# Gathering an expert's tokens in blocks of 32 slots and turning them on VectorE, in an attention and expert-routing kernel

## The chip, the cores and the metric

The kernel runs on one core of a Trainium2 chip. The metric is the device time of one execution in microseconds. The profile is one execution recorded by the hardware profiler. Engine names in it: PE is TensorE's matrix multiply, PEld its weight load, DVE is VectorE, ACT is ScalarE, POOL is GpSimd, SP is SyncE (a trailing q is that engine's queue of DMA issues and waits).

## What is computed

Two blocks follow each other. The first is attention with a threshold, for 8 batches of 8 heads of 576 positions of 64 numbers; its output is laid out as 4608 tokens of 512 numbers (8 heads beside each other). The second sends each token to one of 8 experts, picked by a hash of its id, and puts it through two matrix products.

```python
scores = scale * np.matmul(q, k.transpose(0, 1, 3, 2))
thresh = np.max(scores, axis=-1, keepdims=True) - tau
scores = np.where(scores >= thresh, scores, -1000000000.0)
attn = np.exp(scores - np.max(scores, axis=-1, keepdims=True))
attn = attn / (np.sum(attn, axis=-1, keepdims=True) + 1e-09)
x = np.matmul(attn, v)              # then to (4608, 512)
expert_idx = token_ids * np.int64(2654435761) % np.int64(8)
for e in range(8):
    xe = x[expert_idx == e]
    out[expert_idx == e] = np.maximum(xe @ w1[e], 0.0) @ w2[e]
```

All of it is float32; w1[e] is 512 x 1024 and w2[e] is 1024 x 512. With these inputs the experts get 598, 596, 571, 565, 599, 533, 570 and 576 tokens.

## The kernel before

*Attention* walks over 32 pairs of heads: 4 head pairs (`hp`), each for 8 batches, head pair outermost. A pair has five steps (`s` 0 to 4), and `n = 5 * pair + s` counts them to `LAST` = 160. The order of the instructions inside a step is written out by hand. A step computes scores on TensorE (L214), negates them and takes their minimum on VectorE (`negate`, L225), adds the threshold on GpSimd (`thr`, L232), takes the exponential on ScalarE (L239), masks and sums on VectorE (`mask`, L250), and one to two steps later turns the weights on TensorE (L261) and multiplies with v (L292). At step 0, two pairs later, `put_xm` (L331) divides by the sums on VectorE, and SyncE's queue writes the pair's 576 rows of 128 columns to memory (L337, L342): into `xa_scratch` (columns of the first three head pairs, 384 wide) or `xb_scratch` (the fourth, 128 wide).

*Routing* runs in small pieces between attention's steps. `route` gives each token a slot: expert e owns CAP = 610 slots. `scatters` writes the token numbers into two slot tables in memory (L478), loads them back (L488) and merges them on VectorE (L494) into `gidx`: for each expert five columns of token numbers, one column for each tile of tokens (three of 128 rows, two of 113). A table entry without a token holds a large number, which the gathers pass over.

*Gathers.* `fetch` brings the rows of one tile of one expert from `xa_scratch` or `xb_scratch` into a buffer `xg` by an indirect DMA issued from GpSimd (L104), tokens on partitions. The `xa` parts of experts 0 and 1 are fetched between attention's steps from step `G0` = 130 on, when all writes to `xa_scratch` have been issued. The `xb` parts of both follow the last attention step.

*Turning.* The first product needs the 512 features on partitions. For expert 0 this is done at the end of attention (`early_xT`, L545), and its first product is started there (`early_h`, `late_h`). For experts 1 to 7 `turn_x` does it: four TensorE transposes a tile into PSUM (L722) and one VectorE copy to `xT` (L724).

*Experts.* For each expert e: `gemm1` (L731; 8 groups of 2 x 4 matmuls with 305 tokens as columns; its ReLU goes by turns to ScalarE, L737, and VectorE, L739); then the load of w1 and the ten gathers for expert e+2 (whose buffers are free again); then the second product of e, among which the turns of expert e+1 are spread. `gemm2_last` (L757) computes the last 226 slots with features on partitions, `gemm2` (L745) the first 384 with tokens on partitions, and `turn_last` (L768) turns the former back on TensorE. Each tile of output is copied by ScalarE (L773) and scattered to its rows of the output by an indirect DMA from GpSimd (`store`, L774), each waiting for the one before, as all write the same tensor at places known only at run time. Tokens over an expert's capacity would go through a loop at the end; with these inputs it runs zero times.

The order around the change, in the expert loop, is:

```python
gemm1(e)
load_w1(e + 2); fetch tiles of e + 2
turn_x(e + 1, 0); turn_x(e + 1, 1)
gemm2_last(e)
for kt in range(3):
    turn_x(e + 1, kt + 2)
    gemm2(e, kt)
    turn_last(3 + kt)   # kt = 0, 1
load_w2(e + 2)
```

Of the kernel before, what the change touches and what calls it, by code (L numbers as in the profile page):

```python
# [20 lines left out]
def kernel(  # L21
# [34 lines left out]
    KT, KF, TL = 5, 3, 113  # L56
    TROWS = [P] * KF + [TL] * (KT - KF)
    FIRST = [sum(TROWS[:k]) for k in range(KT)]
    CAP = sum(TROWS)
# [9 lines left out]

    slot_dram = [nc.dram_tensor(f"slot_scratch_{i}", (NSLOT, 1), I32, kind="Internal").ap()  # L70
                 for i in range(2)]

    XA = DIN - P
    xa_dram = nc.dram_tensor("xa_scratch", (N, XA), FP32, kind="Internal").ap()
    xb_dram = nc.dram_tensor("xb_scratch", (N, P), FP32, kind="Internal").ap()
# [16 lines left out]
    drop = consts.tile([P, 1], FP32, name="drop")  # L92
    gidx = consts.tile([P, E, KT], I32, name="gidx")
    gidx_odd = consts.tile([P, E, KT], I32, name="gidx_odd")
# [3 lines left out]
    xg_bufs = [consts.tile([P, DIN], FP32, name=f"xg_{i}") for i in range(2 * KT)]  # L98
# [4 lines left out]
    def gather(x_dram, dst, idx):  # L103
        nc.gpsimd.indirect_dma_start(  # L104
            out=dst, out_offset=None, in_=x_dram[:, :],
            in_offset=bass.IndirectOffsetOnAxis(ap=idx, axis=0),
            bounds_check=N - 1, oob_is_err=False)

    def fetch(e, kt, part):
        xg = xg_bufs[(e * KT + kt) % (2 * KT)]  # L110
        dram, dst = (xa_dram, xg[:, 0:XA]) if part == 0 else (xb_dram, xg[:, XA:DIN])
        gather(dram, dst, gidx[:, e, kt:kt + 1])

    def load_w1(e):
        w1_sb = w_pool.tile([P, CO, F], FP32, name="w1_sb")
        nc.sync.dma_start(out=w1_sb[:], in_=w1[e].rearrange("(c p) f -> p c f", p=P))
        w_tiles[e, 1] = w1_sb
# [6 lines left out]
    with tc.tile_pool(name="a_q", bufs=1) as a_q, \  # L124
# [188 lines left out]
        def x_place(p):  # L313
            hp, b = divmod(p, B)
            return (xa_dram, b * S, hp * P) if hp < HP - 1 else (xb_dram, b * S, 0)
# [10 lines left out]
        def put_xm(p):  # L326
# [9 lines left out]
            x_dram, r0, c0 = x_place(p)  # L336
# [136 lines left out]
        placed = []  # L473

        def scatters():

            for c in range(NTC):
                nc.gpsimd.indirect_dma_start(  # L478
                    out=slot_dram[c % 2][:, :],
                    out_offset=bass.IndirectOffsetOnAxis(ap=slot_i[:, c:c + 1], axis=0),  # L480
                    in_=tok[:, c:c + 1], in_offset=None, bounds_check=NSLOT - 1,
                    oob_is_err=False)
                yield
            for _ in range(4):
                yield
            for table, dst in zip(slot_dram, (gidx, gidx_odd)):
                for p0, p1, k in ((0, TL, KT), (TL, P, KF)):
                    nc.sync.dma_start(  # L488
                        out=dst[p0:p1, :, 0:k],
                        in_=bass.AP(tensor=table.tensor, offset=p0 * KT,  # L490
                                    ap=[[k, p1 - p0], [CAP, E], [1, k]]))
            for _ in range(4):
                yield
            nc.vector.tensor_tensor(out=gidx[:], in0=gidx[:], in1=gidx_odd[:], op=ALU.min)  # L494
# [31 lines left out]
        def constants():  # L526
# [7 lines left out]
            nc.gpsimd.memset(gidx_odd[:], BIG)  # L534
# [4 lines left out]
        def early_xT(tr, k0, k1, c0, c1):  # L539
# [8 lines left out]
            for ka, kb in ((k0, min(k1, KF)), (max(k0, KF), k1)):  # L548
# [43 lines left out]
        G0 = NS * ((HP - 1) * B + 2)  # L592
        pieces, scatter_pieces = route(), scatters()
# [6 lines left out]
        with tc.manual_schedule():  # L600
# [7 lines left out]
            for n in range(LAST + NS + 1):  # L608
# [13 lines left out]
                if s == 1 and 3 <= p < 2 + len(xg_bufs):  # L622
                    nc.sync.dma_start(out=xg_bufs[p - 2][:], in_=xg_bufs[0][:])
                q = p - 1
# [67 lines left out]

                g = n - G0
                if 0 <= g < 2 * KT:
                    fetch(g // KT, g % KT, 0)
                if n == LAST:
                    fill(1)
            for g in range(2 * KT):
                fetch(g // KT, g % KT, 1)
# [6 lines left out]
    with tc.tile_pool(name="m_x", bufs=1) as m_x, \  # L706
# [7 lines left out]
        o_bufs = [m_o.tile([P, DIN], FP32, name=f"o_{i}") for i in range(KT)]  # L714
        oT_sb = m_o.tile([P, CO, CAP - FIRST[KF]], FP32, name="oT_sb")
# [48 lines left out]
        def turn_last(kt, idx):  # L764
            o_ps = ps_x.tile([P, CO, P], FP32, name="xT_ps")
            s0 = FIRST[kt] - FIRST[KF]
            for co in range(CO):
                nc.tensor.transpose(o_ps[0:TL, co, :], oT_sb[:, co, s0:s0 + TL], ident[:])  # L768
            store(o_ps[:].rearrange("p c d -> p (c d)"), kt, idx, TL)
# [8 lines left out]
        def turn_x(e, kt):  # L778
            put_xT(xg_bufs[(e * KT + kt) % (2 * KT)], xT_bufs[e % 2], kt, TROWS[kt])

        with tc.manual_schedule():
            for e in range(E):
                if e > 0:
                    gemm1(w_tiles.pop((e, 1)), xT_bufs[e % 2], h_bufs[e % 2], 2, CH)
                if e + 2 < E:
                    load_w1(e + 2)
                    for g in range(2 * KT):
                        fetch(e + 2, g // 2, g % 2)
                w2_sb = w_tiles.pop((e, 2))
                if e + 1 < E:  # L790
                    turn_x(e + 1, 0)
                    turn_x(e + 1, 1)
                gemm2_last(w2_sb, h_bufs[e % 2])
                for kt in range(KF):
                    if e + 1 < E:
                        turn_x(e + 1, kt + 2)
# [8 lines left out]
        with tc.For_i(0, n_ov, 1) as it:  # L805
# [15 lines left out]
            gather(xa_dram, xg_bufs[0][:, 0:XA], idx[:, 0:1])  # L821
            gather(xb_dram, xg_bufs[0][:, XA:DIN], idx[:, 0:1])
# [37 lines left out]
```

## Time and profile before

| | before |
|---|---|
| time, median of 3 | 1026.33 us (1025.42 to 1027.76) |
| span of the profiled execution | 1025.3 us |
| TensorE clock granted, mean | 0.996 |
| busy: PE, DVE, ACT, POOL | 98%, 49%, 44%, 31% of the span |
| attention, to its last write issued | about 475 us |
| one expert, gemm1 to gemm1 (L731 of experts 1 and 2) | 536.02 to 604.70 us |
| TensorE transposes of turn_x (L722) | 140, busy 19.1 us |
| copies of turned tokens (L724) | 35, busy 22.6 us |
| gathers (L104), experts 0 to 7 | 80, about 1.0 us each on GpSimd |
| stores (L774) | 40, 0.98 us each on GpSimd |

The profile's page has a line of busy times, a map of 40 slices of the span with the busy tenths of each engine, and groups of instructions by source line: times they occur, busy time, mean length of one, and how long the engine stood idle just before them and for whom. The view of stretches gives the busy time of each engine between two times. The timeline lists instructions in order of time, with start, length and count.

### The profile page before, as it was taken

Reading aid. Unit: us, or ns where it says so; the run is one execution under the profiler, and the core shown is the slowest. Engines: PE = TensorE matmul, PEld = TensorE weight load, DVE = VectorE, ACT = ScalarE, POOL = GpSimd, SP = SyncE. Lnnn points to the kernel's source line nnn. Section 1 sums busy time; section 2 is a strip of 40 time slices with the busy share of each in tenths; the row PEclk is TensorE's granted clock in tenths of the full one; section 3 lists DMA queues with packets and bytes.
Section 4 is the critical chain, followed back from the end, with each engine's and each line's share of the span. In section 5 each row is a group of like instructions: output and inputs, shape, how many; then the busy total and the mean of one; then the engine's idle time right before and its main releaser. Section 6 shows DMA issues by size and latency. Waiting matters only on the chain. (4 is left out here: it accounts for less than half of the span.)

```text
span 1025.3 us, 20443 instructions
## 1 busy us (share of the span) xinstructions
PE 1007.2 (98%) x7752; PEld 672.2 (66%) x7752; DVE 507.1 (49%) x1353; ACT 451.8 (44%) x737; POOL 316.4 (31%) x431
## 2 busy tenths in 40 slices
PE   8999999999999999999999999999999999999995
PEld 4666666666666666666857757668577577685772
DVE  7999999999999999983300101001001010010000
ACT  5888888888888988880210010000100100101001
POOL 3233332677773356322413041050140310101001
PEclk9999999999999999999999999999999999999998
DMA  7345554445565598311313241142042412300001
GB/s 178 84 113 138 137 123 114 94 111 118 118 186 155 141 250 197 82 33 27 131 42 133 82 154 43 81 153 82 35 139 82 143 40 93 108 1 37 10 1 47
DMA packets 92146, 103.50 MB, mean 101 GB/s; under 512 B 24709, under 2 KB 65788, under 8 KB 92048
## 3 DMA queue, kind: packets, MB, share of 16 engines
q1 hardware_dynamic: 83424, 83.06, 29.9%
q0 software_dynamic: 8192, 18.91, 5.5%
q8 instruction: 63, 1.03, 0.4%
q14 instruction: 35, 0.29, 0.1%
q10 hardware_dynamic: 432, 0.21, 0.1%
HBM read 81.87 MB, written 20.01 MB: 99 GB/s over the span
## 5 line engine op out<-in xcount | busy, mean ns | idle before, releaser
L239 ACT ACTIVATE w<-ns,nmx 128x576 f32<-128x576 f32 x288 | 220.3, 776 | 34.7 <-DVE ns L225 34.6
L731 PE MATMUL sc<-xT,w_sb 128*128 128x305 f32 x896 | 231.2, 419 | 0.0
L250 DVE SCALAR_TENSOR_TENSOR w<-ns,thr,w 128x576 f32<-128x576 f32 x288 | 226.0, 817 | 0.0
L731 PEld LDWEIGHTS sc<-xT,w_sb 128*128 128x128 f32 x896 | 169.3, 189 | 63.2 <-issue 3.3
L225 DVE TENSOR_SCALAR_CACHE_REDUCE ns<-sc 128x576 f32<-128x576 f32 x288 | 205.4, 746 | 6.2 <-PE sc L214 5.5
L214 PE MATMUL sc<-k_sb,q 64*128 64x288 f32 (+1 forms) x1280 | 178.9, 423 | 1.3 <-DVE k_sb L523 0.7
L745 PE MATMUL o_ps<-w_sb,h 128*128 128x512 f32 x384 | 168.9, 593 | 0.0
L774 POOL DMA_INDIRECT out_dram<-o,gidx x40 | 39.5, 987 | 409.0 <-ACT o L773 350.8
L261 PEld LDWEIGHTS tr<-ident,w 64*128 64x128 f32 x2624 | 107.0, 139 | 88.7 <-ACT wT_b L282 26.3
L232 POOL TENSOR_SCALAR thr<-nmx,drop 128x2 f32<-128x2 f32 (+1 forms) x160 | 102.3, 639 | 188.6 <-DVE ns L225 176.6
L739 DVE TENSOR_SCALAR h<-sc 128x610 f32<-128x610 f32 x28 | 22.2, 794 | 257.3 <-PE sc L731 257.3
L261 PE MATMUL tr<-ident,w 64*128 64x64 f32 x2624 | 139.4, 231 | 2.5 <-ACT wT_a L282 2.0
L745 PEld LDWEIGHTS o_ps<-w_sb,h 128*128 128x128 f32 x384 | 71.3, 190 | 80.3 <-issue 80.3
L724 DVE COPY xT<-xT_ps 128x512 f32<-128x512 f32 (+1 forms) x35 | 22.6, 662 | 179.3 <-PE xT_ps L722 179.3
L214 PEld LDWEIGHTS sc<-k_sb,q 64*128 64x128 f32 (+1 forms) x1280 | 93.2, 177 | 23.2 <-DVE ns L225 9.3
L292 PE MATMUL av<-wT_a,v 128*64 128x320 f32 (+1 forms) x704 | 100.8, 419 | 0.0
L737 ACT ACTIVATE h<-sc 128x610 f32<-128x610 f32 x28 | 19.0, 679 | 182.7 <-PE sc L731 182.7
L757 PE MATMUL sc<-h,w_sb 128*128 128x226 f32 x512 | 99.0, 353 | 0.0
L757 PEld LDWEIGHTS sc<-h,w_sb 128*128 128x128 f32 x512 | 96.2, 189 | 1.1
L282 ACT COPY wT_a<-tr 128x512 f32<-128x512 f32 (+1 forms) x128 | 81.7, 638 | 20.1 <-PE tr L261 19.6
L282 ACT COPY wT_b<-tr 128x512 f32<-128x512 f32 (+1 forms) x128 | 81.2, 635 | 9.3 <-PE tr L261 6.9
L292 PE MATMUL av<-wT_b,v 128*64 128x256 f32 x640 | 83.2, 389 | 0.0
(105 smaller groups left out, 607.4 us busy)
## 6 DMA issues: line engine op xcount, KB each, us to landing
w_sb<-in_moe_w_dram SPq DMA_DIRECT2D x16, 2048.0 KB
q<-in_q_dram SPq DMA_DIRECT2D x62, 288.0 KB
v<-in_v_dram SPq DMA_DIRECT2D x32, 256.0 KB
xa_scratch<-xm SPq DMA_DIRECT2D x24, 256.0 KB
k_sb<-in_k_dram SPq DMA_DIRECT2D x31, 144.0 KB
k_sb<-in_k_dram SPq DMA_DIRECT2D x32, 112.0 KB
xg<-xg SPq DMA_DIRECT2D x9, 256.0 KB
xb_scratch<-xm SPq DMA_DIRECT2D x8, 256.0 KB
```

The costliest lines, as they stand in the source:

```text
L214: nc.tensor.matmul(sc[out_rows, i, 0:S2], lhsT=q_sb[rows, h, q0:q1], rhs=k_sb[rows, h], start=True, stop=True)
L225: nc.vector.tensor_scalar(out=ns[:].rearrange("p (i s) -> p i s", i=2), in0=sc[:, :, 0:S2], scalar1=-1.0, scalar2=None, op0=ALU.mult, op1= ...
L232: nc.gpsimd.tensor_scalar(out=thr[:, 0:j + 1], in0=stats[n][0][:, 0:j + 1], scalar1=drop[:], scalar2=None, op0=ALU.add)
L239: nc.scalar.activation(w, nss[n, j][:], AF.Exp, bias=stats[n][0][:, j:j + 1], scale=-1.0)
L250: nc.vector.scalar_tensor_tensor(out=w, in0=nss.pop((n, j))[:], scalar=stats[n][1][:, j:j + 1], in1=w, op0=ALU.is_le, op1=ALU.mult, accum_ ...
L261: nc.tensor.transpose(dst[:, r, 64 * c:64 * c + 64], src[rows, c0:c0 + P], ident[rows, rows])
L282: nc.scalar.copy(dst, tr[:, :, 0:64 * n_c].rearrange("p r (c q) -> p r c q", c=n_c))
L292: nc.tensor.matmul(av[64 * j:64 * j + 64, g, c0:c1], lhsT=v_sb[:, c, 64 * j:64 * j + 64], rhs=wT[g][:, i, c0:c1], start=(c == 0), stop=stop)
L731: nc.tensor.matmul(h_ps[:, i, 0:width], lhsT=w1_sb[:, co, fo * P:fo * P + P], rhs=xT[:, co, i * width:i * width + width], start=(co == 0), ...
L745: nc.tensor.matmul(o_ps[0:rows], lhsT=h_sb[:, fo, FIRST[kt]:FIRST[kt] + rows], rhs=w2_sb[:, fo, :], start=(fo == 0), stop=(fo == FO - 1))
L757: nc.tensor.matmul(oT_ps[:, i, c * width:c * width + width], lhsT=w2_sb[:, fo, co * P:co * P + P], rhs=h_sb[:, fo, FIRST[KF]:CAP], start=( ...
L774: nc.gpsimd.indirect_dma_start(out=out[:, :], out_offset=bass.IndirectOffsetOnAxis(ap=idx, axis=0), in_=o_sb[:], in_offset=None, bounds_ch ...
```

## The change

The tokens of experts 1 to 7 are gathered in another shape, so that VectorE can turn them in squares of 32 x 32. The 608 slots of an expert (CAP is 32 x 19 now) are taken as 19 blocks of 32 slots. One gather fills one block on all 128 partitions: partitions 32h to 32h+31 hold the 32 tokens of the block, with the 128 numbers of head pair h. All 32 x 32 squares of that block, turned in place, then leave features on partitions: partition 32h+a of chunk j holds feature 128h + 32j + a. That is not the order in which w1's rows were loaded, so the rows of w1 are loaded in that order, by four DMAs of 32 partitions each. Expert 0 keeps its order, its turning by TensorE and its w1.

What follows from it: the two tensors `xa_scratch` and `xb_scratch` become one, `x_scratch`, of which a row of 128 numbers is one token's head pair, and a gather's index is 4 times the token plus the head pair. The slot tables are loaded four times, once for every 32 partitions (`stok`), and the indices of expert 0's tiles (`gidx_0`), of the stores (`gidx`) and of the blocks (`gidx_x`) are derived on VectorE. As a gather by the one tensor may touch any column, the fourth head pair's columns are filled once in early attention. Expert 0's first three head pairs are fetched by 15 gathers of 128 columns at steps 2, 3 and 4 of the last pairs; expert 1 and 2's blocks only after attention. The tiles of the second product become four of 128 and one of 96 rows.

```diff
-    KT, KF, TL = 5, 3, 113
-    TROWS = [P] * KF + [TL] * (KT - KF)
-    FIRST = [sum(TROWS[:k]) for k in range(KT)]
-    CAP = sum(TROWS)
+    KT, KF, NB = 5, 3, 19
+    CAP = 32 * NB
+    FIRST = [P * k for k in range(KT)]
+    TROWS = [P] * (KT - 1) + [CAP - FIRST[-1]]
...
-    xa_dram = nc.dram_tensor("xa_scratch", (N, XA), FP32, kind="Internal").ap()
-    xb_dram = nc.dram_tensor("xb_scratch", (N, P), FP32, kind="Internal").ap()
+    x_dram = nc.dram_tensor("x_scratch", (N, DIN), FP32, kind="Internal").ap()
+    x_rows = x_dram.rearrange("n (h d) -> (n h) d", h=HP)
...
+    def fetch_0(kt, hp):
+        gather(x_rows, xg_bufs[kt][:, P * hp:P * hp + P], gidx_0[:, kt, hp:hp + 1])
     def load_w1(e):
         w1_sb = w_pool.tile([P, CO, F], FP32, name="w1_sb")
-        nc.sync.dma_start(out=w1_sb[:], in_=w1[e].rearrange("(c p) f -> p c f", p=P))
+        if e == 0:
+            nc.sync.dma_start(out=w1_sb[:], in_=w1[e].rearrange("(c p) f -> p c f", p=P))
+        else:
+            for h in range(HP):
+                nc.sync.dma_start(
+                    out=w1_sb[32 * h:32 * h + 32],
+                    in_=w1[e, P * h:P * h + P].rearrange("(c a) f -> a c f", a=32))
...
-            for table, dst in zip(slot_dram, (gidx, gidx_odd)):
-                for p0, p1, k in ((0, TL, KT), (TL, P, KF)):
...
+            for table, dst in zip(slot_dram, (stok, stok_odd)):
+                for h in range(HP):
                     nc.sync.dma_start(
+                        out=dst[32 * h:32 * h + 32],
+                        in_=table[0:E * CAP].rearrange("(e c s) o -> c e (s o)", e=E, c=32))
...
-            nc.vector.tensor_tensor(out=gidx[:], in0=gidx[:], in1=gidx_odd[:], op=ALU.min)
+            nc.vector.tensor_tensor(out=stok[:], in0=stok[:], in1=stok_odd[:], op=ALU.min)
+            for h in range(4):
+                rows, n = slice(32 * h, 32 * h + 32), (NB - h + 3) // 4
+                nc.vector.tensor_copy(gidx[rows, :, 0:n], stok[rows, :, h::4])
...
+            for h in range(HP):
+                nc.vector.tensor_scalar(out=gidx_0[:, :, h], in0=gidx[:, 0], scalar1=float(HP),
+                                        scalar2=float(h), op0=ALU.mult, op1=ALU.add)
...
+            nc.vector.tensor_scalar(out=gidx_x[:], in0=stok[:], scalar1=float(HP),
+                                    scalar2=head[:], op0=ALU.mult, op1=ALU.add)
...
-                if s == 1 and 3 <= p < 2 + len(xg_bufs):
+                if s == 1 and 3 <= p < 2 + KT:
                     nc.sync.dma_start(out=xg_bufs[p - 2][:], in_=xg_bufs[0][:])
+                if s == 1 and 2 + KT <= p < 2 + KT + N // DIN:
+                    r0 = DIN * (p - 2 - KT)
+                    nc.sync.dma_start(
+                        out=x_dram[r0:r0 + DIN, DIN - P:].rearrange("(t p) m -> p t m", p=P),
+                        in_=xg_bufs[0][:].rearrange("p (t m) -> p t m", m=P))
...
-                g = n - G0
-                if 0 <= g < 2 * KT:
-                    fetch(g // KT, g % KT, 0)
+                if n >= G0 and s > 1 and early:
+                    fetch_0(*early.pop(0))
...
-            for g in range(2 * KT):
-                fetch(g // KT, g % KT, 1)
+            for kt in range(KT):
+                fetch_0(kt, HP - 1)
...
+        xb_bufs = [m_x.tile([P, NB, P], FP32, name=f"xb_{i}") for i in range(2)]
...
-        def turn_x(e, kt):
-            put_xT(xg_bufs[(e * KT + kt) % (2 * KT)], xT_bufs[e % 2], kt, TROWS[kt])
+        def fetch(e):
+            for i in range(NB):
+                gather(x_rows, xb_bufs[e % 2][:, i], gidx_x[:, e, i:i + 1])
+        def turn_x(e):
+            for s0, s1 in ((0, NB // 2), (NB // 2, NB)):
+                nc.vector.transpose(
+                    out=xT_bufs[e % 2][:, :, 32 * s0:32 * s1].rearrange(
+                        "p j (s c) -> p s j c", c=32),
+                    in_=xb_bufs[e % 2][:, s0:s1].rearrange("p s (j a) -> p s j a", a=32))
         with tc.manual_schedule():
+            for e in (1, 2):
+                nc.gpsimd.memset(xb_bufs[e % 2][:], 0.0)
+                fetch(e)
             for e in range(E):
                 if e > 0:
                     gemm1(w_tiles.pop((e, 1)), xT_bufs[e % 2], h_bufs[e % 2], 2, CH)
                 if e + 2 < E:
                     load_w1(e + 2)
-                    for g in range(2 * KT):
-                        fetch(e + 2, g // 2, g % 2)
+                    if e > 0:
+                        fetch(e + 2)
                 w2_sb = w_tiles.pop((e, 2))
                 if e + 1 < E:
-                    turn_x(e + 1, 0)
-                    turn_x(e + 1, 1)
+                    turn_x(e + 1)
                 gemm2_last(w2_sb, h_bufs[e % 2])
                 for kt in range(KF):
-                    if e + 1 < E:
-                        turn_x(e + 1, kt + 2)
                     gemm2(w2_sb, h_bufs[e % 2], kt, gidx[:, e, kt:kt + 1], P)
```

## The prediction

> **What bounds the kernel now.** I read the page first, then the busy time by stretches, then TensorE's instructions in order of time in one middle expert and in the last expert, and then GpSimd's and SyncE's instructions in order of time where attention ends.
>
> From the page (engine totals, then busy tenths in 40 slices, then two groups of its costliest list):
> ```profile
> PE 1007.2 (98%) x7752; PEld 672.2 (66%) x7752; DVE 507.1 (49%) x1353; ACT 451.8 (44%) x737; POOL 316.4 (31%) x431
> PE   8999999999999999999999999999999999999995
> DVE  7999999999999999983300101001001010010000
> ...
> L774 POOL DMA_INDIRECT out_dram<-o,gidx x40 | 39.5, 987 | 409.0 <-ACT o L773 350.8
> ...
> L724 DVE COPY xT<-xT_ps 128x512 f32<-128x512 f32 (+1 forms) x35 | 22.6, 662 | 179.3 <-PE xT_ps L722 179.3
> ```
> There are two stages. Up to about 455 us TensorE and VectorE are both full; after it TensorE alone is. The same by stretches (attention, experts 1 to 6, expert 7; columns: length, then busy us of each engine):
> ```profile
> 20.00:455.00 435.00, 434.00 (x5390) 273.98 (x5390) 429.84 (x1209) 380.10 (x620) 198.36 (x293) 1.00 0.52 130
> 536.02:948.09 412.07, 412.07 (x1610) 289.69 (x1609) 37.91 (x54) 38.17 (x60) 80.14 (x80) 1.00 0.25 88
> ```
> So in attention VectorE is busy 429.84 of 435 us: an instruction added to it there moves the end by about its length. In the expert stage TensorE has no gap and VectorE works 9% of the time: what leaves TensorE there comes off the end, and VectorE can take ten times its present work.
>
> TensorE in order of time, first expert 1, which turns expert 2's tokens, then expert 7, which has none to turn (start, length):
> ```profile
> 536.02 33.03 PE L731 MATMUL sc<-xT,w_sb 128*128 128x305 f32 x128
> 568.89 1.03 PE L722 MATMUL xT_ps<-ident,xg 128*128 128x128 f32 x8
> 569.76 12.38 PE L757 MATMUL sc<-h,w_sb 128*128 128x226 f32 x64
> 581.98 0.60 PE L722 MATMUL xT_ps<-ident,xg 128*128 128x128 f32 x4
> 582.41 7.03 PE L745 MATMUL o_ps<-w_sb,h 128*128 128x512 f32 x16
> ...
> 590.11 7.04 PE L745 MATMUL o_ps<-w_sb,h 128*128 128x512 f32 x16
> ```
> ```profile
> 948.09 33.03 PE L731 MATMUL sc<-xT,w_sb 128*128 128x305 f32 x128
> 980.96 12.38 PE L757 MATMUL sc<-h,w_sb 128*128 128x226 f32 x64
> 993.17 7.03 PE L745 MATMUL o_ps<-w_sb,h 128*128 128x512 f32 x16
> ...
> 1000.47 7.03 PE L745 MATMUL o_ps<-w_sb,h 128*128 128x512 f32 x16
> ```
> Expert 7 is the experiment already made: the same matmuls without the twenty L722 turns. I take start-to-start times, since matmuls overlap and their lengths (272 ns for a turn) overstate what they cost.
>
> [...] no VectorE turn is in this trace. [...] 685 ns for 512 elements (L724, the full form). [...] the quickest land 2.5 us after issue. [...] The 113-row load of that table (L488) holds SyncE's queue for 11.66 us[...].
>
> **Part 1, the turns leave TensorE.** Per expert with turns, from the lines above: L731 to L757 takes 33.74 us with, 32.87 without: 0.87. L757 to the first L745 takes 12.65 against 12.21: 0.44. First to second L745 takes 7.70 against 7.30: 0.40, and the third the same again, 0.40. Sum 2.1 us. Seven experts' tokens are turned so (1 to 7): 7 x 2.1 = 14.7 us off the end.
>
> **Part 2, 608 slots in place of 610.** L731 runs at 32.87/128 = 0.257 us for 305 columns, 0.84 ns a column: one column less in 896 matmuls is 0.75 us. L757 runs at 12.21/64 = 191 ns for 226 columns, so two columns less would be 1.7 ns x 512 = 0.86 us; but the weight load takes 189 ns and may become the bound, so between 0 and 0.9. I take 0.75. Together 1.5 us. The largest expert has 599 tokens, so 608 slots overflow no more than 610 did, and the loop at the end stays empty.
>
> **Part 3, VectorE turns instead.** Per expert two instructions of 9 x 128 = 1152 and 10 x 128 = 1280 elements per partition. At the 1.3 ns an element of L724 that is 1.5 + 1.7 us; [...] I take 2.8 and bound it by four times that, 11 us. All are hidden: between L731's end and the next L731 VectorE has some 35 us with nothing else in it (it did the L724 copies there, which go), and TensorE reads the result only at the next L731. The last L739 goes ahead of the turn in program order, as before.
>
> **Part 4, gathers: 19 a expert in place of 10.** The row that prices them is L104; three in order of time where attention ends:
> ```profile
> 477.77 1.10 POOL L104 DMA_INDIRECT xg<-xb_scratch,gidx  x1 [19.41 <-DMA xb_scratch<-xm]
> 479.17 1.02 POOL L104 DMA_INDIRECT xg<-xb_scratch,gidx  x1 [0.30 <-issue]
> 480.50 1.01 POOL L104 DMA_INDIRECT xg<-xb_scratch,gidx  x1 [0.30 <-issue]
> ```
> These already have the new form, 128 rows of 512 bytes: one per 1.31 us. Nineteen take 24.9 us. Behind them on GpSimd queue only the five stores (L774), each 1 us plus a wait for the store before it, 3.4 to 3.8 us apart, 18 us. That is 43 of some 66 us an expert: hidden. The gather for expert e+2 follows gemm1 of e and is read a whole expert later, so its landing is hidden too.
> The one tight place is the first. Nothing of expert 1 can be fetched before the last attention write has landed, since a block now spans all four head pairs; before, three quarters of it were there already. From 477.8: five gathers for expert 0 to 484.3, a fill of the block buffer (2432 elements; GpSimd fills 288 in 338 ns and 128 in 204, so 0.84 ns each, 2.1 us), nineteen gathers to 511.3, landing 2.5, second turn 1.7: 515.5 us. TensorE wants it at 536.0 minus the 2.1 of turns gone, about 533.9. It has 18 us to spare. Expert 2's gathers then end near 538 and expert 0's stores go out behind them, up to 17 us late; five output buffers take them, and the next use of those is near 585. Hidden.
>
> **Part 5, attention.** VectorE gains 4 copies and 4 small scalings (around 0.14 us each by pitch; rows of that size show 146 to 192 ns, overlapping a little), one scaling of 152 elements (0.25), and the minimum grows from 40 to 152 elements (+0.12): 1.5 us, all on the path. GpSimd has 15 gathers in place of 10, at 1.36 us, one for each of three steps in five; it runs at 70% with scatters at the same pace elsewhere without slowing attention. The 9 fills of the fourth head pair's columns lie beside everything else on SyncE's queue, which is ahead of need.
> A new wait: one tensor now holds all head pairs, so a gather waits for the attention write of the current pair, which it did not before. Behind it on GpSimd is thr (L232), and VectorE's mask (L250) waits for thr. In the usual pair the write lands before the gather's turn (written 403.3 to 405.3, DMA quiet by 407; turn 407). In the pair after the second w2 load it is late: written 392.45 to 394.04 behind 2 MB, turn at 393.23, so 2 to 4 us of wait. thr has about 2.7 us to spare there (next mask 4.97 us after the gather's turn, minus 1.36 gather, 0.73 thr and queueing). I add 0.5 us. Moving 64 KB a gather where 192 KB went helps this write.
>
> **Sum.** 1026.3 - 14.7 - 1.5 + 1.5 + 0.5 = **1012.1 us**.
>
> **Rivals.** *Stalls in attention* (15%): every pair from 26 to 30 waits for its write as pair 27 does, some 2 us on VectorE each: 5 x 2 = 10, 1022 us. For: VectorE has no slack. Against: four of the five writes land in time by the trace. *Expert 1 comes late* (8%): it takes a gather pitch over 2.2 us; at 2.6 TensorE waits 19 x 1.3 - 18 = 7 us: 1019. Against: 1.31 is measured for this very form. *Gathers one at a time, as the stores are* (5%): if writes into one block buffer wait for each other, 3.5 us each, 19 take 67 and with the stores 85 us against an expert's 66: five experts 19 us late, about 1105, slower. Against: the two gathers into one xg buffer, at different columns, do not wait today. *Forecast* (72%).
>
> **How the numbers follow.** Low end: no cost in attention and the whole of part 2, 1026.3 - 14.7 - 1.6 = 1010, and half a microsecond for the spread of runs: 1009.5. High end: forecast plus a few waits in attention, or a late expert 1: 1019. This leaves out the serial gathers and most of the first rival. Faster 0.93, same 0.02, slower 0.05 (the serial case).
>
> **What would show it.** Right: no L722 and no L724; L757 starting 32.8 us after L731 in every expert; an expert about 66.3 us long (68.67 before); no gap on TensorE before expert 1's first L731; gathers 1.3 us apart. Attention up to its last write longer by 1 to 3 us. Wrong: a gap before an L731 released by the VectorE turn (then gathers or turns are late); GpSimd waits on attention writes with VectorE idle for thr behind them; stores in wait behind gathers with TensorE idle.

## The result and the profile after

| | before | after |
|---|---|---|
| time, median of 4 runs each, side by side | 1026.41 us (1025.42 to 1027.76) | 1032.39 us (1031.36 to 1033.03) |
| ratio, 95% interval | | 1.0056 (1.0039 to 1.0074) |
| span of the profiled execution | 1025.3 us | 1031.4 us |
| one expert, first product to first product | 68.67 us | 66.33 us |
| start of expert 0's second product (L757, L793) | 501.08 us | 525.86 us |
| TensorE clock granted, mean | 0.996 | 0.986 |

The changed kernel is 6 us slower where 14.2 us less were forecast. The page of after answers to the lines shown of before: engine totals, TensorE and VectorE by fortieths of the span, and three groups (line, engine, operation, output <- input; busy us and mean ns; idle before).

```profile
PE 997.2 (97%) x7612; PEld 660.5 (64%) x7612; DVE 504.6 (49%) x1341; ACT 451.1 (44%) x735; POOL 393.4 (38%) x509
...
PE   7999999999999999999299999999999999999997
...
DVE  7999999999999999973120110100101001010000
...
L775 DVE TENSOR_SCALAR h<-sc 128x608 f32<-128x608 f32 x28 | 22.2, 791 | 426.2 <-PE sc L767 426.2
...
L810 POOL DMA_INDIRECT out_dram<-o,gidx x40 | 39.4, 985 | 323.4 <-ACT o L809 225.9
L109 POOL DMA_INDIRECT xb<-x_scratch,gidx_x x133 | 133.3, 1002 | 40.5 <-issue 38.4
```

TensorE's work shrank by 10 us, but its row now has a 2 where every slice had been 9 (the twentieth slice, about 490 to 516 us). The view by stretches puts numbers on it (columns: length, then busy us of PE, PEld, DVE, ACT and POOL; then granted clock, DMA share, GB/s). The rows are expert 0's part, its second product, and two whole experts:

```profile
478.00:525.90 47.90, 29.13 (x106) 19.65 (x104) 12.83 (x15) 5.28 (x11) 35.32 (x34) 0.79 0.17 49
525.90:559.50 33.60, 33.60 (x121) 22.01 (x121) 0.79 (x1) 4.29 (x7) 14.20 (x15) 1.00 0.46 112
559.50:625.80 66.30, 66.30 (x249) 46.31 (x248) 5.84 (x6) 6.34 (x10) 23.96 (x24) 1.00 0.35 100
625.80:692.20 66.40, 66.40 (x250) 46.34 (x249) 5.84 (x6) 6.34 (x10) 23.95 (x24) 1.00 0.35 100
```

The experts are what was forecast: 66.3 us, TensorE without a gap. The loss is in the first row alone, 18.8 us without TensorE. The timeline of after there, TensorE first and then VectorE (start, length, instruction, and in brackets how long the engine idled before it and for whom):

```profile
492.69 2.21 PE L595 MATMUL sc<-xT,w_sb 128*128 128x304 f32 x8
502.91 2.36 PE L609 MATMUL sc<-xT,w_sb 128*128 128x304 f32 x4 [8.01 <-DVE h L599]
516.03 9.99 PE L609 MATMUL sc<-xT,w_sb 128*128 128x304 f32 x28 [10.76 <-DVE h L599]
525.86 1.36 PE L793 MATMUL sc<-h,w_sb 128*128 128x224 f32 x6
```
```profile
500.71 1.38 DVE L822 STREAM_TRANSPOSE xT<-xb 128x1152 f32<-128x1152 f32 x1 [11.94 <-DMA xb<-x_scratch,gidx_x]
502.01 0.75 DVE L599 COPY h<-sc 128x608 f32<-128x608 f32 x1
513.78 1.51 DVE L822 STREAM_TRANSPOSE xT<-xb 128x1280 f32<-128x1280 f32 x1 [11.02 <-DMA xb<-x_scratch,gidx_x]
515.22 0.75 DVE L599 COPY h<-sc 128x608 f32<-128x608 f32 x1
515.90 0.77 DVE L613 TENSOR_TENSOR h<-h,sc 128x608 f32<-128x608 f32 x1
```

Read it from TensorE backwards. L609, the last quarter of expert 0's first product, waits for L599, a VectorE copy that empties a PSUM buffer. L599 waits for nothing of its own: it stands in VectorE's queue behind L822, the new turn of **expert 1's** tokens, and L822 waits for expert 1's gathers. The eight additions L613 of expert 0 stand behind both turns. In this trace neither of the last two L599 goes ahead of the turn before it in that queue, though VectorE stands idle for 11.94 and 11.02 us until the turn starts: they start 0.08 and 0.07 us before the turn's record ends (502.01; 500.71 + 1.38, and 515.22; 513.78 + 1.51).

That is not the order of the kernel's text. L599 and L613 belong to the first ordered region (attention and expert 0's first product), L822 to the second (the expert loop). Within each region VectorE's instructions run here in the order of the text, but on the engine the two regions are merged; by which rule, no run shows. For expert 0's part the queue is six of the eight L599, then L822, L599, L822, L599, and eight times L613. The kernel before had the same merging, at no cost, since what came early there waited for nothing long: the output buffers' fills, text of the second part, ran among expert 0's copies.

```profile
465.56 0.79 DVE L572 COPY h<-sc 128x610 f32<-128x610 f32 x1 [6.95 <-PE sc L568]
470.49 2.11 DVE L717 MEMSET o<- 128x512 f32 x4 [4.13 <-PE av L292]
472.56 0.79 DVE L572 COPY h<-sc 128x610 f32<-128x610 f32 x1
```

### The profile page after: what moved, and what is told of

Same layout as the page of the kernel before. It is cut to its first block, busy times and chain, and to the rows that moved or that the text cites. A ratio compares the mean times of both kernels' runs of the same rounds, so it can differ in the third digit from the quotient of the medians.

```text
span 1031.4 us, 20338 instructions
## 1 busy us (share of the span) xinstructions
PE 997.2 (97%) x7612; PEld 660.5 (64%) x7612; DVE 504.6 (49%) x1341; ACT 451.1 (44%) x735; POOL 393.4 (38%) x509
## 2 busy tenths in 40 slices
DMA packets 97666, 104.66 MB, mean 101 GB/s; under 512 B 26270, under 2 KB 71854, under 8 KB 97568
## 5 line engine op out<-in xcount | busy, mean ns | idle before, releaser
L775 DVE TENSOR_SCALAR h<-sc 128x608 f32<-128x608 f32 x28 | 22.2, 791 | 426.2 <-PE sc L767 426.2
L767 PE MATMUL sc<-xT,w_sb 128*128 128x304 f32 x896 | 230.4, 419 | 0.0
L109 POOL DMA_INDIRECT xb<-x_scratch,gidx_x x133 | 133.3, 1002 | 40.5 <-issue 38.4
L773 ACT ACTIVATE h<-sc 128x608 f32<-128x608 f32 x28 | 19.0, 677 | 182.0 <-PE sc L767 182.0
L793 PE MATMUL sc<-h,w_sb 128*128 128x224 f32 x512 | 98.2, 353 | 0.0
L793 PEld LDWEIGHTS sc<-h,w_sb 128*128 128x128 f32 x512 | 96.8, 190 | 1.2 <-issue 0.3
```

Of the source, the lines that this page charges most:

```text
L109: nc.gpsimd.indirect_dma_start(out=dst, out_offset=None, in_=src, in_offset=bass.IndirectOffsetOnAxis(ap=idx, axis=0), bounds_check=src.sh ...
L767: nc.tensor.matmul(h_ps[:, i, 0:width], lhsT=w1_sb[:, co, fo * P:fo * P + P], rhs=xT[:, co, i * width:i * width + width], start=(co == 0), ...
L793: nc.tensor.matmul(oT_ps[:, i, c * width:c * width + width], lhsT=w2_sb[:, fo, co * P:co * P + P], rhs=h_sb[:, fo, FIRST[KF]:CAP], start=( ...
```

## The experiments

**Theory**: the two turns at the head of VectorE's queue cost all of the gain and 6 us more. **Rivals**: the half clock that followed TensorE's idleness is a large part of it; one of the two turns does it alone; the 133 gathers slow the other engines.

The runs fell on five chips of two kinds. On three of them the kernel before takes 1026 us, on the other two 1042 (1041.48 and 1042.46, within 3 us of it in every run). Each of the five ran in one stretch of time only, so whether the chip or that stretch makes the difference isn't separated; "chip" stands for both below. Every time is compared only with the kernel before on the same chip; times are medians of 4 or 5 runs (of 1 for the kernel before as a run of its own).

| run | before there | this | ratio (95%) |
|---|---|---|---|
| e1_turn_behind | 1042.46 | 1079.89 | 1.036 (1.034 to 1.0379) |
| e2_fill_gap | 1042.46 | 1101.65 | 1.0561 (1.0545 to 1.0577) |
| e3_half_behind | 1042.46 | 1082.30 | 1.0387 (1.0357 to 1.0417) |
| e4_double_gathers | 1042.46 | 1266.46 | 1.2142 (1.2123 to 1.216) |
| before_again | 1026.46 | 1026.74 | one run |
| after_again | 1026.46 | 1033.20 | 1.0064 (1.0046 to 1.0081) |
| e1_again | 1026.46 | 1009.00 | 0.9835 (0.9819 to 0.9852) |
| e5_spread_gathers | 1026.46 | 1010.77 | 0.9841 (0.9825 to 0.9858) |
| e2_again | 1041.48 | 1105.39 | 1.059 (1.0545 to 1.0634) |
| e3_again | 1041.48 | 1084.71 | 1.04 (1.0343 to 1.0456) |
| e4_again | 1041.48 | 1266.31 | 1.2165 (1.213 to 1.22) |
| e6_no_gathers | 1041.48 | 1047.56 | 1.0061 (1.0039 to 1.0084) |
| before_third | 1026.67 | 1027.92 | one run |
| after_third | 1026.67 | 1033.16 | 1.0069 (1.0052 to 1.0085) |
| e3_third | 1026.67 | 1018.64 | 0.9935 (0.9916 to 0.9954) |
| e5_third | 1026.67 | 1011.50 | 0.9846 (0.9825 to 0.9867) |
| e2_third | 1026.62 | 1033.22 | 1.0056 (1.0037 to 1.0075) |
| after_fourth | 1026.62 | 1033.40 | 1.0064 (1.0044 to 1.0084) |

### Both turns behind expert 0's additions

The decisive edit names the last addition, and lets expert 1's two turns be queued only after it. All else stays.

```diff
-                nc.vector.tensor_tensor(out=h3, in0=h3, in1=h_ps[:, :, 0:CH], op=ALU.add)
+                added = nc.vector.tensor_tensor(out=h3, in0=h3, in1=h_ps[:, :, 0:CH], op=ALU.add)
...
+            return added
...
-            late_h()
+            last_add = late_h()
...
-                    turn_x(e + 1)
+                    if e == 0:
+                        with tc.issue_after(last_add.ins):
+                            turn_x(1)
+                    else:
+                        turn_x(e + 1)
```

Its first run fell on a chip of 1042, and contradicted the theory:

> Only the order of VectorE's queue changes: the two turns of expert 1 stand behind the last addition of late_h instead of ahead of it. Queue theory (the turns wait for the gathers of expert 1 at the head of VectorE's queue, and late_h behind them starves TensorE): expert 0's gemm2_last starts near 503.5 us instead of 525.9, TensorE has no gap over 1 us there, the clock stays at full speed, and the time is 1032.4 - 22.4 = 1010, with the experts at 66.3 us each as before. Rival one (the gathers of expert 1 are simply too late): the gap moves to just ahead of expert 1's gemm1, some 15 us of it, and the time stays over 1024. Rival two (the granted clock falls for another reason, such as more DMA or VectorE work): the clock stays near 0.986 and the time over 1028.

1079.89 us; where the time goes on such a chip is the subject of the last experiments. Run again beside both kernels, with the rival that the new order itself delays something:

> The kernel before, for its trace beside the other runs of this call. Theory A (the 1079.9 us of the kernel with the turns queued behind is owed to that chip: there TensorE's semaphore updates reach the other engines late while GpSimd issues gathers): if this call lands on such a chip, 1042 us, and the ReLUs of experts 2 to 6 show late updates in the burst of ten gathers; if it lands on the chip of the first pair, 1026 us and none. Theory B (the delay comes from the new instruction order): no late update here in either case.

> The changed kernel as it is. Theory A: 1032 us where the kernel before takes 1026; some 1095 to 1105 us where the kernel before takes 1042 (19 gathers for each expert, each late ReLU as in the kernel with the turns behind, and expert 0's 25 us stall on top). Theory B: 1032 us beside 1026, or 1048 beside 1042, in experts 2 to 7 always the exact pace of 66.3 us.

> The turns of expert 1 queued behind expert 0's additions, once more, for the chip. Theory A: beside 1026 us for the kernel before, 1009 to 1012 us (the 24.8 us between expert 0's additions and its second product fall to some 2, and nothing else moves); beside 1042, 1080 us again. Theory B: 1064 us beside 1026, and 1080 beside 1042.

On this chip (before 1026.46) it takes 1009.0 us: 24.2 less than the changed kernel beside it and 17.5 less than the kernel before. The timeline of after_again, TensorE, and of e1_again, TensorE and then VectorE (a turn is L823 in e1_again; its line numbers after L613 are one higher than in after):

```profile
492.16 3.34 PE L595 MATMUL sc<-xT,w_sb 128*128 128x304 f32 x12
...
526.77 3.44 PE L793 MATMUL sc<-h,w_sb 128*128 128x224 f32 x17
```
```profile
489.23 3.34 PE L595 MATMUL sc<-xT,w_sb 128*128 128x304 f32 x12
492.40 8.85 PE L609 MATMUL sc<-xT,w_sb 128*128 128x304 f32 x32
501.09 12.33 PE L794 MATMUL sc<-h,w_sb 128*128 128x224 f32 x64
```
```profile
500.14 0.79 DVE L613 TENSOR_TENSOR h<-h,sc 128x608 f32<-128x608 f32 x1 [0.24 <-PE sc L609]
501.29 0.79 DVE L613 TENSOR_TENSOR h<-h,sc 128x608 f32<-128x608 f32 x1 [0.36 <-PE sc L609]
501.99 1.37 DVE L823 STREAM_TRANSPOSE xT<-xb 128x1152 f32<-128x1152 f32 x1
516.23 1.51 DVE L823 STREAM_TRANSPOSE xT<-xb 128x1280 f32<-128x1280 f32 x1 [12.86 <-DMA xb<-x_scratch,gidx_x]
```

The second turn still waits 12.86 us for its gathers and starts no earlier than in after (516.23; 513.78 in the first profile). But nothing urgent stands behind it now. The price of the order is the distance from the last twelve matmuls of L595 to the second product: 501.09 - 489.23 = 11.86 us here, 526.77 - 492.16 = 34.61 in after_again. That is **22.75 us** for the two turns, waits and slower clock together. The rival of a harmful new order falls.

### Only the second turn behind

`turn_half` is one of the two turns by itself; `last_add` is the last addition, as above.

```diff
+        def turn_x(e, after=None):
+            turn_half(e, 0, NB // 2)
+            if after is None:
+                turn_half(e, NB // 2, NB)
+                return
+            with tc.issue_after(after.ins):
+                turn_half(e, NB // 2, NB)
...
-                    turn_x(e + 1)
+                    if e == 0:
+                        turn_x(1, last_add)
+                    else:
+                        turn_x(e + 1)
```

> Only the second turn behind expert 0's additions. Where the kernel before takes 1026: 1018 to 1021 us if each of the two turns holds VectorE by itself; 1030 to 1032 if one wait takes over what the other gives up; 1009 if the second turn alone did it. Where it takes 1042: 1078 to 1085 again.

1018.64 us beside 1033.16 for after_third. The timeline of e3_third, TensorE:

```profile
488.94 3.34 PE L595 MATMUL sc<-xT,w_sb 128*128 128x304 f32 x12
500.26 10.35 PE L609 MATMUL sc<-xT,w_sb 128*128 128x304 f32 x32 [7.99 <-DVE h L599]
510.45 12.33 PE L794 MATMUL sc<-h,w_sb 128*128 128x224 f32 x64
```

One wait is left, the first, at its old length (7.99 us; 8.01 in after). The distance is 510.45 - 488.94 = 21.51 us: 9.65 above e1_again for the first turn, and 13.1 more with the second. So the two add up, and neither does it alone. The same kernel's two earlier runs fell on the chips of 1042 (1082.30 and 1084.71 us), where other delays cover it:

> Only the second of the two turns of expert 1 stands behind late_h; the first, which waits for 9 gathers, stays ahead of it. Queue theory: the first gap of 8.0 us stays, the second of 10.8 goes, and the matmuls after the first gap run at half clock for up to 20 us, which costs another 3 us: 1010 + 8 + 3 = 1021. Rival (late gathers): no change from the changed kernel, 1032.

> Only the second of expert 1's two turns queued behind expert 0's additions. Each turn holds VectorE by itself in my theory (11.9 us before the first, 11.0 before the second): beside 1026 us for the kernel before, some 12 us of the 24.8 stay, 1018 to 1021 us. If one wait takes over what the other gives up: 1030 to 1032. Beside 1042: 1080 again.

### TensorE kept busy in the wait

The changed kernel, with transposes of the identity matrix (their result is not used) ahead of the first two groups:

```diff
             for fo in range(FO):
                 h_ps = ps_sc.tile([P, 2, 512], FP32, name="sc")
+                for _ in range((58, 78, 0)[min(fo, 2)]):
+                    nc.tensor.transpose(av[:, 0, 0:P], ident[:], ident[:])
```

> The changed kernel with the 58 and 78 identity transposes on TensorE in its wait. Where the kernel before takes 1026 us: 1028 to 1029 (the wait stays, the half clock goes) if the half clock follows from TensorE's idleness; 1033 if not. Where it takes 1042: 1100 again.

1033.22 us beside 1033.40 for after_fourth: no gain, where 4 to 5 us were expected. The stretches 496 to 505, 505 to 515 and 515 to 530 us, of after_fourth and then of e2_third (the clock is the third column from the right):

```profile
496.00:505.00 9.00, 2.36 (x4) 1.17 (x4) 2.06 (x2) 0.00 (x0) 6.87 (x8) 0.56 0.18 50
505.00:515.00 10.00, 0.00 (x0) 0.00 (x0) 1.46 (x2) 0.00 (x0) 8.21 (x8) 0.50 0.14 38
515.00:530.00 15.00, 14.21 (x50) 10.71 (x51) 6.94 (x10) 5.68 (x8) 11.34 (x13) 0.80 0.34 83
```
```profile
496.00:505.00 9.00, 7.32 (x63) 6.86 (x62) 2.05 (x2) 0.00 (x0) 7.04 (x7) 1.00 0.19 50
505.00:515.00 10.00, 9.58 (x82) 9.03 (x81) 0.00 (x0) 0.00 (x0) 8.00 (x8) 1.00 0.19 52
515.00:530.00 15.00, 12.02 (x43) 8.87 (x44) 8.40 (x10) 5.68 (x8) 11.68 (x12) 0.89 0.23 60
```

The clock stayed up as long as the fill lasted (1.00 and 1.00 for 0.56 and 0.50), so idleness is what brought it down. It did not stay up to the end (0.89 in the last stretch). The fill had run out while TensorE still waited for the second turn, as e2_third's timeline shows:

```profile
505.90 8.68 PE L609 MATMUL av<-ident 128*128 128x128 f32 x78
517.98 9.37 PE L611 MATMUL sc<-xT,w_sb 128*128 128x304 f32 x28 [3.40 <-DVE h L599]
```

After these 3.40 us the clock fell to half once more, from 519.37 to 522.78 us, among the 28 matmuls. In after_fourth it is at half from 497.00 to 520.89 us, of which the 5.1 us from 515.78 on lie among the 28 matmuls, and the rest where TensorE mostly waited. So the fill saved 1.7 us of half clock among them. The distance from L595 to the second product fell from 525.81 - 491.21 = 34.60 to 527.18 - 493.45 = 33.73 us, 0.87 us, about half of 1.7. The clock fell 5.4 us after TensorE's last matmul in after and 2.4 us after it in after_fourth, where it came back 5.1 us after the 28 matmuls began. What half clock does to matmuls shows in the first four L609: 2.36 us in after_fourth, where it is granted, and 1.26 in e2_third at 1.00. Half of the time at half clock is then an estimate of the loss. Over all 23.9 us that would be 12 us; over the 5.1 us in which TensorE had matmuls to run it is 2.6 us. The 28 matmuls come near the second figure: from the first of them to the second product are 525.81 - 515.78 = 10.03 us in after_fourth, and 7.60 by the pace of the 32 in e1_again (501.09 - 492.40 = 8.69 us), 2.4 less. The 0.87 us for 1.7 fits that reading too: time at half clock in which the engine waits anyway costs nothing. So the half clock makes up an estimated 2.6 of the 22.75 us, of which this run won back 0.87; no run with this wait kept the clock up to the end of it.

The baselines of these two comparisons were expected so, and came out at 1033.16 and 1033.40 us:

> The changed kernel. On a chip where the kernel before takes 1042: 1080 to 1105 us, experts 1 to 5 at 72 to 75 us, 6 and 7 at 66.3. On a chip where it takes 1026: 1032.5 and 66.33 everywhere.

> The changed kernel. Where the kernel before takes 1026: 1033 again, beside which the other run of this call is read. Where it takes 1042: 1080 to 1105, experts 1 to 5 at 72 to 75 us, 6 and 7 at 66.3.

Two earlier runs of the edit fell on the chips of 1042 (1101.65 and 1105.39 us), and tell nothing of the half clock. Since the fill changes nothing on the chip of 1026, they are the nearest to a time of the changed kernel on a chip of 1042. On the same chip as the first of them the kernel with both turns behind took 1079.89 us, so an estimated 22 us are won there too:

> The changed kernel with 58 and 78 idle transposes of the identity put on TensorE ahead of the first and the second group of late_h, where it stood idle for 8.0 and 10.8 us; the queue of VectorE is as in the changed kernel. It separates waiting from the half clock that follows it. Queue theory: the second group still starts near 516 us, since VectorE releases it, and only the slow matmuls after it come back to full speed (28 of them in 7.8 us instead of 10.0): 1032.4 - 2.2 = 1030. Rival (the half clock is the loss, the waiting hardly matters): below 1024.

> The changed kernel with 58 and 78 identity transposes on TensorE ahead of the first two groups of expert 0's last product, which fill its wait. If the 24.8 us are the wait for the two turns plus the half clock that TensorE's idleness brings: on a chip where the kernel before takes 1026 us, no half clock about 500 us, the wait unchanged, and 1028 to 1029 us beside the 1032.5 of the changed kernel (4 us less). If the half clock has another cause, 1032.5. On a chip where the kernel before takes 1042: 1100 again.

### The gathers, and the chips of 1042

The third rival was tried in both directions from the kernel of e1_turn_behind. Doubled: each gather of experts 1 to 7 is issued again into a buffer that nobody reads.

```diff
             for i in range(NB):
                 gather(x_rows, xb_bufs[e % 2][:, i], gidx_x[:, e, i:i + 1])
+            for i in range(NB):
+                gather(x_rows, xd[:, i], gidx_x[:, e, i:i + 1])
```

> The first experiment's kernel with each gather of experts 1 to 7 issued a second time into a buffer that nobody reads: 38 gathers an expert, 38 x 1.31 + 18 for the stores = 68 us of GpSimd's queue against an expert's 66.3. Theory (19 gathers are hidden with room to spare): within 2 us of the first experiment, about 1011, since the backlog grows by only 2 us an expert. Rival (the gathers press on the expert stage through DMA or GpSimd's queue): over 1016.

> As the kernel with both turns behind (1009.0), with every gather of experts 1 to 7 issued a second time into a buffer that nobody reads: 38 of 1.31 us for each expert, 50 us of GpSimd's 66. If gathers lie beside TensorE as the prediction had it: within 4 us of 1009 beside 1026 (expert 1 comes 25 us later and may cost up to 10 more, since its second turn would then end at some 541 where the product wants it at 535). If gathers slow TensorE here too: over 1050. On the chip of 1042: 1266 again.

Both runs fell on the chips of 1042 and took 1266 us. On the chips of 1026 the doubling was not tried. Taken away: the gathers of experts 3 to 7 are left out, whose products then use older tokens.

```diff
                 if e + 2 < E:
                     load_w1(e + 2)
-                    if e > 0:
-                        fetch(e + 2)
```

> As the kernel with both turns behind, without the gathers of experts 3 to 7, whose products then run on older data (so the output is not the reference's): the dose below. Hidden gathers: 1009 within 1 us beside 1026. On the chip of 1042, if it is the gathers that delay TensorE's updates there: experts 1 to 5 at 66.3 us each, 40 us below the kernel with the turns behind, 1035 to 1045; if it is something else there, 1080.

1047.56 us, just above the 1035 to 1045 expected, and experts of 66.33 us, as expected. What happens on such a chip is seen in expert 1's first product. Of e1_turn_behind, TensorE, ScalarE (ReLU of groups 1, 3 and 5) and VectorE (groups 2, 4 and 6), and then ScalarE of e6_no_gathers:

```profile
571.40 20.63 PE L768 MATMUL sc<-xT,w_sb 128*128 128x304 f32 x80
593.86 4.36 PE L768 MATMUL sc<-xT,w_sb 128*128 128x304 f32 x16 [1.83 <-DVE h L776]
601.58 4.77 PE L768 MATMUL sc<-xT,w_sb 128*128 128x304 f32 x11 [3.36 <-ACT h L774]
```
```profile
575.70 0.68 ACT L774 ACTIVATE h<-sc 128x608 f32<-128x608 f32 x1 [3.51 <-PE sc L768]
583.88 0.68 ACT L774 ACTIVATE h<-sc 128x608 f32<-128x608 f32 x1 [7.51 <-PE sc L768]
600.85 0.68 ACT L774 ACTIVATE h<-sc 128x608 f32<-128x608 f32 x1 [16.29 <-remote]
```
```profile
579.79 0.79 DVE L776 TENSOR_SCALAR h<-sc 128x608 f32<-128x608 f32 x1 [50.37 <-issue]
593.02 0.79 DVE L776 TENSOR_SCALAR h<-sc 128x608 f32<-128x608 f32 x1 [12.43 <-PE sc L768]
601.01 0.79 DVE L776 TENSOR_SCALAR h<-sc 128x608 f32<-128x608 f32 x1 [7.20 <-remote]
```
```profile
585.81 0.68 ACT L774 ACTIVATE h<-sc 128x608 f32<-128x608 f32 x1 [7.51 <-PE sc L768]
594.00 0.68 ACT L774 ACTIVATE h<-sc 128x608 f32<-128x608 f32 x1 [7.51 <-PE sc L768]
602.18 0.68 ACT L774 ACTIVATE h<-sc 128x608 f32<-128x608 f32 x1 [7.51 <-PE sc L768]
```

ReLUs should come every 8.19 us on each engine, and do without gathers. With them the fourth and fifth groups, whose matmuls are recorded up to 592, get their ReLU at 593.02 and 600.85. The ReLUs wait for TensorE's semaphore update, and the trace has those updates at 592.99, 600.83 and 600.99 us, the last of 19 gathers being issued at 597.25. Experts 1 to 5 take 72.4 to 75.0 us in e1_turn_behind, the sixth, with no gather in its time, 66.33. On the other of the two chips experts 1 to 5 take 72 to 75 us with 19 gathers each (e3_again), every one takes 66.33 without gathers (e6_no_gathers), and with twice as many several take 100 (e4_again).

The experts are only half of the loss. The profiled execution of e1_turn_behind is 73.6 us longer than that of e1_again: 6.1 us of it come before the last twelve L595, 30.5 between them and expert 1's first product, and 36.9 in experts 1 to 5. The 30.5 us fall where the 38 gathers of experts 1 and 2 are issued (491 to 543 us), which e6_no_gathers keeps, and there TensorE waits for VectorE and starts single matmuls late as well. Of e1_turn_behind, TensorE, the second product of expert 0, which takes 24.5 us (12.2 in e1_again):

```profile
525.44 7.29 PE L794 MATMUL sc<-h,w_sb 128*128 128x224 f32 x36
533.06 0.35 PE L794 MATMUL sc<-h,w_sb 128*128 128x224 f32 x1 [0.33 <-issue]
...
549.93 7.03 PE L782 MATMUL o_ps<-w_sb,h 128*128 128x512 f32 x16
```

So on these chips it is the gathers that hold TensorE up or make its updates late in the experts; for expert 0 only their coincidence in time is shown. The whole run moves the same 97,666 packets as on a chip of 1026, and GpSimd issues the gathers at the same pace, one per 1.31 us. On the chips of 1026 the experts keep their 66.33 us through the gathers. Why the chips differ stays open. The changed kernel itself was not timed on a chip of 1042: in all four of its timings the kernel before took 1026 us beside it. By e1_turn_behind the idea is a loss there even with the queue in order, 3.6%.

The last variant spreads those gathers: four after the first product, three after each of the five stores.

```diff
-                        fetch(e + 2)
+                        fetch(e + 2, 0, 4)
...
                     gemm2(w2_sb, h_bufs[e % 2], kt, gidx[:, e, kt:kt + 1], P)
+                    if 0 < e < E - 2:
+                        fetch(e + 2, 4 + 6 * kt, 7 + 6 * kt)
                     if kt < KT - KF:
                         turn_last(KF + kt, gidx[:, e, KF + kt:KF + kt + 1])
+                        if 0 < e < E - 2:
+                            fetch(e + 2, 7 + 6 * kt, 10 + 6 * kt)
```

> As the one above, with the 19 gathers of experts 3 to 7 not issued in one burst but four after the first product and three after each of the five stores of the expert. If TensorE's updates come late only in long bursts of gathers: on a chip with the delay 20 to 35 us less than the kernel with the turns behind (its experts 1 to 5 take 72 to 75 us there, the two without gathers 66.3). If every gather delays what TensorE does in its time, no less, since the number of gathers is the same. On a chip without the delay: equal to the kernel with the turns behind within 2 us.

> Both turns behind, the gathers of experts 3 to 7 spread over the expert. Where the kernel before takes 1026: 1010 again. Where it takes 1042: 1080 if every gather delays TensorE wherever it lies; 1050 to 1065 if it is a long burst in the first product that does it (its updates are needed every 4.1 us there, and every 7.3 us in the second product).

Both runs fell on chips of 1026: 1010.77 and 1011.50 us, experts of 66.33 us as with the burst. Whether spreading helps on the other chips is open. The kernel before, traced once more beside e5_third, has its 68.67 us an expert there. Where its 16 us go on the other chips was not traced.

> The kernel before, for its trace in this call. On a chip where it takes 1042 us: experts 1 to 5 (those with ten gathers in their time) longer than the 68.67 us that it has where it takes 1026, 1 to 3 us each, and the last two at 68.67; the rest of the 16 us beside expert 0. If the 16 us came from elsewhere (attention, weights), all experts at 68.67. On a chip where it takes 1026: 68.67 everywhere.

## Why the prediction was wrong

- **Parts 1 and 2 were right.** 2.1 us of turns and 0.2 of columns an expert were forecast; the experts fell from 68.67 to 66.33 us, 2.34.
- **Part 3 failed at "All are hidden".** The price was right: 1370 and 1475 ns on average, 2.85 us for the 2.8 that were the author's estimate; the trace of before has no turn by VectorE. What failed is the argument under it, that between L731's end and the next L731 VectorE has nothing else in it, and that what stands ahead in program order goes ahead of the turn. That holds for experts 2 to 7. For expert 1 the turn comes from the second region, L599 and L613 of expert 0 from the first, and the build put the turn ahead of two L599 and all eight L613. The prediction asked who needs the result of the waiting instruction, and not who is queued behind it. The wait that was put at nothing cost 22.75 us. e1_again shows the step: queued as the text has it, the kernel takes 1009.0 us.
- **Part 4 had the times right and the place wrong.** The second turn of expert 1 was to be done at 515.5 us and was, at 515.29, in part by luck: expert 0's last five gathers began at 480.86 and not at 477.8, and the fill of the block buffer, 2.1 us in the sum, was done before them (473.51), out of the way: the second region's text ahead of the first's once more, on GpSimd. The "18 us to spare" were counted up to expert 1's first product, while what stood behind the turn was due from 495 on.
- **Part 5 was near.** 2.0 us were forecast. By the times at which the pairs' outputs are done, after_third loses 2.2 us on before_third in four steps (0.45, 0.81 and 0.14 us at pairs 22, 23 and 25, where the index work stands, and 0.77 at the last), and gains 0.3 over the others. In after and after_again the first three steps are the same, but the last is 2.4 and 2.3 us, so attention loses 3.5 and 3.4 in all. In these two the granted clock stands at half for 3.4 us from about 460 us on, in after_third it does not; the 1.6 us more are about half of that. Why it falls there is open. Waits of gathers for attention's writes sum to 2.9 us inside attention in after and 5.1 in after_third, with no VectorE stall behind them.
- **Of the rivals** none came: attention does not stall, expert 1 is not late for its own gathers, and gathers are not issued one at a time. The case that happened, a wait at the head of a queue that holds up unrelated work, was not among them.
- **With the order mended, 3.1 us better than forecast,** half a microsecond under the range's low end of 1009.5. 2.9 of them come after the last matmul: 10.34 us to the end in before_again, 7.42 in e1_again, where GpSimd's last drain takes 1.47 us for 4.16. The prediction had no term for that, and its cause is not shown.

## What to carry to other kernels

A wait has two prices: who needs its result, and who stands behind it on the same engine. Read the second from the built queue and not from the text, above all where two separately ordered stretches of code meet. If an early instruction of the next stage waits for a transfer, tie it behind the last urgent instruction of the stage before: here that one tie turned 1033.2 us into 1009.0, 1.65% below the kernel before, on a chip of 1026. And where a change trades one resource for many small transfers, time it on more than one chip before relying on the gain.

## What the runs showed of the hardware that was not expected

- On two of five chips, each seen in one stretch of time, the kernel before takes 1.5% longer (1042 us for 1026), and the kernel with both turns behind, which issues 153 gathers in place of 80, 7% longer (1079.89 for 1009.00). There TensorE's semaphore updates arrive up to 8.8 us late during a run of gathers (600.83 us in e1_turn_behind for the fifth group, due at 592.0: the first group's update at 575.67, and four times the 4.09 us between groups in e6_no_gathers).
- TensorE's granted clock went to half 5.4 us after TensorE ran dry in after (at 500.25 us, idle from 494.9) and 2.4 us after it in after_fourth (at 497.00, idle from 494.55), and stayed there for 20.5 and 23.9 us. Keeping it up for part of TensorE's wait won 0.87 us (e2_third beside after_fourth).
- One VectorE instruction that turns 32 x 32 squares of float32 takes 1370 ns for 1152 elements a partition and 1475 for 1280 (L822 of after, means of seven each), 1.15 to 1.19 ns an element.
